# Last row pair of a Strassen-Winograd matmul kernel: another order of the seven products, the residual put into a PSUM bank, and the last copies split over two engines

## Chip, cores and metric

The kernel runs on one core of a Trainium2 chip. The metric is the device time of one execution in microseconds (us). Three runs of the kernel before gave 866.5, 866.58 and 866.75 us, so the median is 866.58 us.

## What is computed

With x of 2048 rows (tokens) by 640 columns (channels):

```python
xn = layernorm(x)                                   # over the 640 channels
a, b = xn @ dft_hid_re.T, xn @ dft_hid_im.T
A = dft_seq_re @ a - dft_seq_im @ b                 # real part of a 2-D Fourier transform
h = layernorm(xn)
u = gelu(einsum("sd,sf->df", h, w1) + b1)           # f = 1728, mixing across tokens
B = (u @ w2 + b2).T                                 # back to 2048 rows, 640 columns
out = x + A + B
```

All in float32. The last stage, which the change touches, is the product with `w2`.

## The kernel before

**Arithmetic.** Each matmul of float32 operands is done in three passes (`three`, L158). An operand is split into a rounded part hi and a rest lo: ScalarE writes hi with a copy (`high`, L149) and VectorE writes lo with a subtraction (`low`, L152). The passes are hi by hi, hi by lo (L161, L162) and lo by hi (L164).

**Row pairs.** The stages after the sequence transform all go through `row_steps` (L851). It takes two rows of tiles of the left matrix at a time and computes a 2 by 2 block of results with seven products instead of eight (Strassen-Winograd). The left matrix comes as four pieces A11, A12, A21, A22; the sums S1 = A21 + A22, S2 = S1 - A11, S3 = A11 - A21 and S4 = A12 - S2 are made by VectorE (`first_sum`, and `s2`, `s3`, `s4` at L1002). The right matrix with its own sums is in SBUF already (`moving`). In the last stage, `down(1, t)` (L1113), a piece is 128 by 384: three chunks of 128 inner indices. The result block is two tiles of 128 output rows by two halves of 320 columns, called c00, c01, c10, c11 here (row, half). Products 2, 3 and 4 are *stacked*: their last inner chunk has only 64 real rows, so its lo is put on the other 64 partitions and its third pass is left out. Such a product has 8 matmuls of 320 columns, the others have 9. For S4 the lower 64 partitions of that chunk are first made a copy of the upper ones by ScalarE, in `fourth` (L990).

**Banks.** P1 to P7 are the products; each goes into a PSUM bank, and some share one: P1, P6 and P7 accumulate one after another in bank z, P5 and P3 in bank y, P2 has bank w, and P4 has bank u in the last pair. Between two products of one bank the intermediate sum is read out (`read`, L922). c01 is P1 + P6, then + (P5 + P3). c11 is (P5), then + (P1 + P6 + P7). c10 is (P1 + P6 + P7), then + P4. c00 is P1 + P2.

**Order of the work.** The schedule is manual: each engine executes its instructions in the order in which the program text issues them. A *step* is one product; `turn_of(i)` (L1224) issues for step i, in this order: loads, reads of the banks that step i - 1 filled, sums, the hi of the piece for step i + 2 (ScalarE), extras, the lo of that piece (VectorE), the list `behind_lo`, and last the matmuls of step i (TensorE). A piece has three buffers. So operands are two steps ahead of TensorE, and a product's bank is read one step behind it. In what follows s is the first step of the last row pair, and turn s + n the turn of its step n.

**The last row pair** is `down(1, 7)`, with `base` given: the 256 rows of the output so far (x + A + half of B), which is read into a buffer beforehand (`before`, L1128), and added to each result by VectorE, so that the final values are written by plain DMAs (`each`, L1122) and not by accumulating ones. Its order before is 1, 5, 2, 6, 3, 7, 4. Its sums are placed by L1005 to L1009: S2 behind the lo of turn s - 1; S4 and then S3 behind the lo of turn s; `fourth` behind the lo of turn s + 1. Its reads are: P1 copied to c00 by ScalarE (L962); c11 = P5 + base (L958); c00 += P2 (L949); c01 = P1 + P6 + base (L958); c01 += P5 + P3 (L949), and c00 += base (L975); c11 += bank z (L949), and c10 = bank z + base (L979); last c10 += P4, in two halves of 160 columns (L954), of which one is stored from SyncE's queue and one from ScalarE's.

Of the kernel before, what the change touches and what calls it, by code (L numbers as in the profile page):

```python
# [14 lines left out]
P = 128  # L15
# [12 lines left out]
H2 = D // 2  # L28
# [49 lines left out]
def fnet_plus_mixer(  # L78
# [30 lines left out]
    nc = tc.nc  # L109
# [35 lines left out]
    for i in range(WARM):  # L145
        n = CH if i < WARM - 5 else P
# [8 lines left out]
    def sub(to, a, b):  # L155
        nc.vector.tensor_sub(to, a, b)  # L156
# [11 lines left out]
    def bank():  # L168
        bank_turn[0] = (bank_turn[0] + 1) % 8
        return psum[bank_turn[0]]  # L170
# [6 lines left out]
    loads, sums, reads, extras, timed, behind_lo = (defaultdict(list) for _ in range(6))  # L177
# [115 lines left out]
    def pair_at(tag):  # L293
        return keep.tile([P, 2, D], F32, name="pair", tag=tag)
# [3 lines left out]
    def part_of(tag, n):  # L298

        def get():  # L300
            if tag not in shared:
                shared[tag] = keep.tile([P, 3, 2, D], F32, name="pairs", tag=tag)
            return shared[tag][:, n]
        return get

    place = {
        "v": lambda: pair_at("v"), "ca": lambda: pair_at("ca"), "cb": lambda: pair_at("cb"),
        "x0": part_of("xb", 0), "x1": part_of("xb", 1), "x2": part_of("xb", 2),
    }
# [536 lines left out]
    def raw_slot(n):  # L846
        k = n if n == D else CH
        raw_turn[k] = (raw_turn[k] + 1) % (raws[k].shape[1] - 1)
        return raws[k][:, raw_turn[k], :n]

    def row_steps(stage, nq, load_piece, at, end, bias=(None, None), base=None, earliest=0, each=None, aside={}, tail=False, stacked=()):  # L851
# [6 lines left out]
        s0, n = len(steps), nq * P  # L858
        raw, banks, held = {}, {}, {}
# [19 lines left out]

        order = (1, 5, 2, 6, 3, 7, 4) if base else (1, 5, 6, 2, 7, 3, 4)

        early = n < D
        loads_of = {-6: ("A11", "A21", "A22"), -4: ("A12",)} if early else {
# [2 lines left out]
        operand = {1: "A11", 5: "s", 6: "A11", 2: "A12", 7: "A21", 3: "A12", 4: "A22"}  # L888
# [7 lines left out]
        new_bank = (1, 5, 2)  # L896
# [2 lines left out]
            new_bank += (7, 3)  # L899
        if base:  # L900
            bank_of[4] = "u"
            new_bank += (4,)
        of_moving = {1: 0, 2: 1, 3: 2, 5: 3, 7: 4, 4: 5, 6: 6}

        goes_to = {1: (0, 0, True), 5: (1, 1, True), 6: (0, 1, True), 2: (0, 0, False), 7: (1, 1, False),
# [16 lines left out]
        def read(i):  # L922
            def run():
                if i == 1:
                    held["c"] = place[at]()
                row, half, fresh = goes_to[i]
                cols = slice(half * H2, (half + 1) * H2)
                c, b = held["c"][:, row, cols], banks[bank_of[i]][:, :H2]
                if tail and i in (5, 7, 4):

                    def upper():
                        aside[i](row, half, b)
                        if i == 4:
                            end(held["c"])


                    if i == 7:
                        upper()
                    else:
                        extras[s0 + (4 if i == 5 else order.index(i) + 1)].append(upper)  # L940
                    if i == 5:
                        nc.scalar.activation(c, b, AF.Copy)
                    else:
                        nc.vector.tensor_add(c[:TAIL], b[:TAIL], c[:TAIL])
                    return
                if i in aside:
                    aside[i](row, half, b)
                elif not fresh:
                    nc.vector.tensor_add(c, b, c)  # L949
                elif base and i == 4:  # L950

                    for k, queue in enumerate((nc.sync, nc.scalar)):
                        of = slice(k * H2 // 2, (k + 1) * H2 // 2)
                        nc.vector.tensor_add(c[:, of], b[:, of], c[:, of])  # L954
                        each(c, row, half, True, of, queue)
                    return
                elif base and i != 1:
                    nc.vector.tensor_add(c, b, base()[:, row, cols])  # L958
                elif bias[row] is not None:
                    nc.scalar.activation(c, b, AF.Identity, bias=bias[row])  # L960
                else:
                    nc.scalar.activation(c, b, AF.Copy)  # L962
                if tail and i == 6:

                    low_row = held["c"][:, 1, :]
                    nc.vector.tensor_add(low_row[:, H2:], b, low_row[:, H2:])
                    extras[s0 + 3].append(lambda: nc.scalar.activation(low_row[:, :H2], b, AF.Copy))
                    p5 = banks["u"][:TAIL, :H2]
                    behind_lo[s0 + 3].append(lambda: nc.vector.tensor_add(c[:TAIL], p5, c[:TAIL]))
                if each:  # L970
                    each(c, row, half, i in (7, 3, 4))
                if base and i == 3:

                    c11 = held["c"][:, 0, :H2]
                    nc.vector.tensor_add(c11, c11, base()[:, 0, :H2])  # L975
                    each(c11, 0, 0, True)
                if base and i == 7:

                    nc.vector.tensor_add(held["c"][:, 1, :H2], b, base()[:, 1, :H2])  # L979
                if i == 4 and not each:  # L980
                    end(held["c"])
            return run

        if stacked:

            def second_time():
                last = raw["s"][:, n - P :]
                nc.scalar.activation(last[TAIL:], last[:TAIL], AF.Copy)

            def fourth():  # L990

                last = raw["A12"][:, n - P :]
                nc.scalar.activation(last[TAIL:], last[:TAIL], AF.Copy)

            if not base:
                extras[s0 + 1].append(second_time)
        for e, names in loads_of.items():
            loads[max(s0 + e, earliest)].append(lambda names=names: load(*names))
        if n == D or stacked:

            operand[6] = "s"
            s2 = lambda: sub(raw["s"], raw["s"], raw["A11"])  # L1002
            s3 = lambda: sub(raw["A21"], raw["A11"], raw["A21"])
            s4 = lambda: sub(raw["A12"], raw["A12"], raw["s"])
            if base:  # L1005
                sums_of = {-2: (first_sum,)}
                behind_lo[s0 - 1].append(s2)
                behind_lo[s0].extend((s4, s3))
                behind_lo[s0 + 1].append(fourth)  # L1009
            elif stacked:  # L1010
                sums_of = {-2: (first_sum,), 2: (s4,)}
                behind_lo[s0 - 1].append(s2)
                extras[s0].append(s3)
            elif s0 == s_hid:

                behind_lo[s0 - 2].append(first_sum)
                sums_of = {0: (s2,), 1: (s3,), 2: (s4,)}
            else:
                sums_of = {-2: (first_sum, s3), 2: (s4,)}
                behind_lo[s0 - 1].append(s2)  # L1020
        elif stage == "down0":

            sums_of[-2] = sums_of[-2][:1]
            behind_lo[s0 - 2].append(lambda: sub(raw["A21"], raw["A11"], raw["A21"]))
# [11 lines left out]
    def hidden(n, t, earliest):  # L1036
        ts = (t, t + 4)

        def load_piece(to, i, j):
            c, b = divmod(ts[i], CH // P)  # L1040
            nc.sync.dma_start(to.rearrange("p (j t) -> p j t", j=ND), y_part[j][c][:, :, b * P : (b + 1) * P])

        return row_steps("hid", ND, load_piece, ("ca", "cb")[n % 2] if n else "c", lambda c: collect(c, ts), earliest=earliest)

    def up(stage, r, at):
# [60 lines left out]
        if tail:  # L1106
            aside += (5, 7, 4)
        s0 = row_steps(
            f"up{stage}", 4, load_piece, at, end, earliest=s_up - 4, aside={i: by_dram(i) for i in aside}, tail=tail,
        )  # L1110
# [137 lines left out]
    with tc.manual_schedule():  # L1248
        for word in START.split():
            start[word[0]](*map(int, word[1:].split("-")))  # L1250
        for i in range(FIRST_STEP, len(steps) + 1):
# [6 lines left out]
            elif i >= s_hid:  # L1258
                k = sum(i >= s for s in (s_up, s_up + 7 * NF2, s_down))
                at, of = LONG_AT[k]  # L1260
# [43 lines left out]
```

## Time and profile before

| | |
|---|---|
| median of 3 runs | 866.58 us (866.5 to 866.75) |
| profiled execution: span from first to last instruction | 865.1 us |
| profiled execution: own time | not recorded apart from the span |
| TensorE busy | 860.7 us, 99% of the span |
| VectorE busy | 695.2 us, 80% |
| ScalarE busy | 523.0 us, 60% |
| granted TensorE clock | 1.000 |

The profile names engines PE (TensorE), PEld (its weight loads), DVE (VectorE), ACT (ScalarE), POOL (GpSimd) and SP (SyncE); a q behind a name is that engine's queue. A timeline row reads: start in us, busy us, engine, line of the kernel, operation, output <- input, shapes, how many instructions are merged in the row (x), and in brackets how long the engine sat idle before it and what ended that. The seven products of the last pair are 60 matmuls (four products of 9, three of 8).

### The profile page before, as it was taken

What the parts mean: (1) busy time and instruction counts of PE and PEld (TensorE: products, weight loads), DVE (VectorE), ACT (ScalarE), POOL (GpSimd) and SP (SyncE); (2) the same over time, 40 slices, a digit from 0 to 9 for tenths busy, and PEclk for the clock granted to TensorE, in tenths of its full rate; (3) what the DMA queues carried; (4) which work ended last, traced back from release to release, by engine and by line L of the source; (5) the groups of instructions that cost most, each with busy time, mean ns of one, the idle gap of its engine ahead of it and who ended that gap; (6) DMA issues with size and microseconds to landing.
All of it is one profiled execution on the core that took longest, in us unless ns stands there. A gap on an engine that the chain in (4) does not pass through costs nothing.

```text
span 865.1 us, 13904 instructions
## 1 busy us (share of the span) xinstructions
PE 860.7 (99%) x4899; PEld 789.6 (91%) x4899; DVE 695.2 (80%) x1177; ACT 523.0 (60%) x968; POOL 158.8 (18%) x215
## 2 busy tenths in 40 slices
PE   9999999999999999999999999999999999999998
PEld 6888888888888888889999999999999999999998
DVE  7898868758767888677877788888679978987887
ACT  5765576763555555547565556676667866555654
POOL 2222131210020211122110101111312221101211
PEclk9999999999999999999999999999999999999999
DMA  9949596695382746869576766665687689766776
GB/s 337 366 103 268 186 245 235 160 292 151 94 191 29 199 102 135 212 107 200 125 167 157 163 138 196 189 173 162 142 185 176 146 241 244 183 141 126 157 170 149
DMA packets 90293, 154.44 MB, mean 179 GB/s; under 512 B 9008, under 2 KB 37424, under 8 KB 89968
## 3 DMA queue, kind: packets, MB, share of 16 engines
q0 software_dynamic: 25008, 57.52, 36.1%
q1 hardware_dynamic: 64928, 95.80, 34.0%
q8 instruction: 38, 0.62, 0.3%
q10 hardware_dynamic: 288, 0.25, 0.1%
q14 instruction: 31, 0.25, 0.1%
HBM read 99.96 MB, written 58.82 MB: 184 GB/s over the span
## 4 chain that ended last, share of the span: by engine, by line
PE 99%; DMA 1%; SPq 0%; ACT 0%; DVE 0%; issue 0%; DVEq 0%
PE psum L161 32%; PE psum L162 32%; PE psum L164 31%; PE psum L515 3%; DMA pieces<-in_dft_seq 1%; ACT piece L150 0%; SPq L503 0%; SPq L539 0%; DVE pair L954 0%; DVEq L1300 0%
## 5 line engine op out<-in xcount | busy, mean ns | idle before, releaser
L153 DVE TENSOR_TENSOR piece<-pieces,piece 128x512 fp32r<-128x512 f32 (+4 forms) x496 | 327.2, 660 | 129.8 <-ACT piece L150 125.2
L150 ACT ACTIVATE piece<-pieces 128x512 fp32r<-128x512 f32 (+3 forms) x472 | 295.3, 626 | 224.6 <-PE psum L164 143.0
L161 PE MATMUL psum<-piece,n 128*128 128x512 f32 x540 | 210.3, 389 | 0.0
L164 PE MATMUL psum<-piece,n 128*128 128x512 f32 x540 | 210.3, 389 | 0.0
L162 PE MATMUL psum<-piece,n 128*128 128x512 f32 x540 | 210.3, 389 | 0.0
L162 PE MATMUL psum<-sup,piece 128*128 128x320 f32 x392 | 120.9, 309 | 0.0
L162 PE MATMUL psum<-sdown,piece 128*128 128x320 f32 x392 | 120.9, 309 | 0.0
L161 PE MATMUL psum<-sup,piece 128*128 128x320 f32 x392 | 120.9, 309 | 0.0
L161 PE MATMUL psum<-sdown,piece 128*128 128x320 f32 x392 | 120.9, 309 | 0.0
L162 PEld LDWEIGHTS psum<-piece,n 128*128 128x128 f32 x540 | 101.4, 188 | 21.1
L161 PEld LDWEIGHTS psum<-piece,n 128*128 128x128 f32 x540 | 101.4, 188 | 20.9
L164 PEld LDWEIGHTS psum<-piece,n 128*128 128x128 f32 x540 | 101.4, 188 | 20.9
L156 DVE TENSOR_TENSOR pieces<-pieces 128x512 f32<-128x512 f32 (+3 forms) x142 | 111.9, 793 | 3.0
L164 PE MATMUL psum<-sup,piece 128*128 128x320 f32 x368 | 113.9, 310 | 0.0
L164 PE MATMUL psum<-sdown,piece 128*128 128x320 f32 x368 | 113.9, 310 | 0.0
L492 POOL DMA_DIRECT2D y<-c x65 | 56.0, 898 | 255.2 <-DVE c L691 154.0
L164 PE MATMUL psum<-shid,piece 128*128 128x320 f32 x280 | 86.7, 310 | 0.0
L162 PE MATMUL psum<-shid,piece 128*128 128x320 f32 x280 | 86.7, 309 | 0.0
L161 PE MATMUL psum<-shid,piece 128*128 128x320 f32 x280 | 86.6, 309 | 0.0
L161 PEld LDWEIGHTS psum<-sdown,piece 128*128 128x128 f32 x392 | 73.6, 188 | 0.0
L161 PEld LDWEIGHTS psum<-sup,piece 128*128 128x128 f32 x392 | 73.6, 188 | 0.0
L162 PEld LDWEIGHTS psum<-sup,piece 128*128 128x128 f32 x392 | 73.6, 188 | 0.0
(135 smaller groups left out, 1107.2 us busy)
## 6 DMA issues: line engine op xcount, KB each, us to landing
pieces<-in_dft_seq SPq DMA_DIRECT2D x120, 256.0 KB, 5.4
y<-c POOLq DMA_DIRECT2D x105, 256.0 KB, 4.9
pieces<-in_w SPq DMA_DIRECT2D x88, 256.0 KB, 3.8
out<-pair POOLq DMA_DIRECT2D x36, 320.0 KB, 5.5
pieces<-y SPq DMA_DIRECT2D x32, 320.0 KB, 4.2
pieces<-in_w SPq DMA_DIRECT2D x32, 192.0 KB, 2.6
out<-in_x SPq DMA_DIRECT2D x16, 320.0 KB, 8.8
up<-pair POOLq DMA_DIRECT2D x8, 640.0 KB, 3.2
```

The costliest lines, as they stand in the source:

```text
L150: nc.scalar.activation(hi, src, AF.Copy)
L153: nc.vector.tensor_sub(lo, src, hi.bitcast(F32))
L156: nc.vector.tensor_sub(to, a, b)
L161: nc.tensor.matmul(psum, wh, mh, start=first, stop=False, skip_group_check=True)
L162: nc.tensor.matmul(psum, wh, ml, start=False, stop=last and wl is None, skip_group_check=True)
L164: nc.tensor.matmul(psum, wl, mh, start=False, stop=last, skip_group_check=True)
L492: nc.gpsimd.dma_start(y_part[m][c][:, j, :], t, accum_op=ALU.add)
L515: nc.tensor.matmul(banks[m, j], channels(k, j)[rows], w[cols], start=n == 0 and k == begin, stop=n == 2 and k == end, skip_group_check=True,)
```

## The change

Only the last row pair (`base`) changes.

- The order becomes 1, 5, 6, 3, 7, 4, 2: P6 moves one step forward to step 2, P3 to step 3, P7 to step 4, P4 to step 5, and P2 goes from step 2 to the end.
- S4 is put in a raw slot of its own instead of over A12, since P2 now needs A12 later than P3 needs S4. It stays behind the lo of turn s, and `fourth`, which now works on the new slot, follows it at once in turn s. S3 moves behind the lo of turn s + 1.
- After P1 has been copied to c00, VectorE writes c00 + base into bank w, behind the lo of turn s + 2 (`seed`). P2 then accumulates onto that (w is no longer among the banks that its first matmul starts anew), so bank w ends as the final c00. The addition of P2 to c00 (L949) and the addition of base to c00 (L975) are gone.
- c10 += P4 is one addition of 320 columns, stored from SyncE's queue, one turn before the end.
- The last thing is now the read of bank w: VectorE copies its first 160 columns to c00, stored from SyncE's queue, and ScalarE copies the other 160 to a place in another buffer, stored from ScalarE's queue.

```diff
-        order = (1, 5, 2, 6, 3, 7, 4) if base else (1, 5, 6, 2, 7, 3, 4)
+        order = (1, 5, 6, 3, 7, 4, 2) if base else (1, 5, 6, 2, 7, 3, 4)
...
         if base:
             bank_of[4] = "u"
-            new_bank += (4,)
+            new_bank = (1, 5, 4)
+            operand[3] = "S4"
...
+                if base and i == 2:
+                    apart = place["x0"]()[:, 0, :H2]
+                    for k, (queue, copy, to) in enumerate(((nc.sync, nc.vector.tensor_copy, c), (nc.scalar, high, apart))):
+                        of = slice(k * H2 // 2, (k + 1) * H2 // 2)
+                        copy(to[:, of], b[:, of])
+                        each(to, row, half, True, of, queue)
+                    return
                 if i in aside:
                     aside[i](row, half, b)
-                elif not fresh:
+                elif not fresh or base and i == 4:
                     nc.vector.tensor_add(c, b, c)
-                elif base and i == 4:
-
-                    for k, queue in enumerate((nc.sync, nc.scalar)):
-                        of = slice(k * H2 // 2, (k + 1) * H2 // 2)
-                        nc.vector.tensor_add(c[:, of], b[:, of], c[:, of])
-                        each(c, row, half, True, of, queue)
-                    return
...
-                if base and i == 3:
-
-                    c11 = held["c"][:, 0, :H2]
-                    nc.vector.tensor_add(c11, c11, base()[:, 0, :H2])
-                    each(c11, 0, 0, True)
...
+                if base and i == 1:
+                    banks["w"] = bank()
+
+                    def seed():
+                        nc.vector.tensor_add(banks["w"][:, :H2], c, base()[:, row, cols])
+
+                    behind_lo[s0 + 2].append(seed)
...
-                last = raw["A12"][:, n - P :]
+                last = raw["S4" if base else "A12"][:, n - P :]
                 nc.scalar.activation(last[TAIL:], last[:TAIL], AF.Copy)
...
+            def s4_apart():
+                raw["S4"] = raw_slot(n)
+                sub(raw["S4"], raw["A12"], raw["s"])
+
             if base:
                 sums_of = {-2: (first_sum,)}
                 behind_lo[s0 - 1].append(s2)
-                behind_lo[s0].extend((s4, s3))
-                behind_lo[s0 + 1].append(fourth)
+                behind_lo[s0].extend((s4_apart, fourth))
+                behind_lo[s0 + 1].append(s3)
```

## Prediction

> **What bounds the kernel now.** I read the page first, then the end of the trace engine by engine. The page:
>
> ```profile
> span 865.1 us, 13904 instructions
> PE 860.7 (99%) x4899; PEld 789.6 (91%) x4899; DVE 695.2 (80%) x1177; ACT 523.0 (60%) x968; POOL 158.8 (18%) x215
> PE 99%; DMA 1%; SPq 0%; ACT 0%; DVE 0%; issue 0%; DVEq 0%
> ```
>
> TensorE is busy for 99% of the span, and the chain that ended last is TensorE throughout. The change leaves the number of matmuls alone, so it can act in two ways only: by making TensorE wait, and through the tail behind the last matmul. Time for three runs is given, none for the profiled execution; its span is 1.48 us below their median (866.58 - 865.1), and I add what changes in the span to 866.58. One per five hundred (1.73 us) is about what can be told from no change here.
>
> TensorE in the last row pair, the first and last of 48 matmuls, and the view by stretches:
>
> ```profile
> 854.72 0.31 PE L161 MATMUL psum<-sdown,piece 128*128 128x320 f32 x1
> ...
> 861.61 0.31 PE L162 MATMUL psum<-sdown,piece 128*128 128x320 f32 x1
> ```
> ```profile
> 855.00:863.00 8.00, 6.92 (x48) 6.66 (x46) 6.84 (x18) 2.22 (x5) 0.21 (x1) 1.00 0.72 142
> ```
>
> 47 intervals in 6.89 us are 0.1466 us a matmul, without a gap, at clock 1.00: a product of 9 lasts 1.32, one of 8 lasts 1.17. Counted back from 861.61 the products begin at 852.96 (P1), 854.28 (P5), 855.60, 856.77, 858.09, 859.26, 860.58. VectorE is busy 6.84 of these 8.00 us, so it has little room to catch up: what matters is when its queue gets to an instruction.
>
> VectorE and ScalarE around the last pair (the pair before it, for the order that the change takes over, begins 8.8 us earlier):
>
> ```profile
> 844.89 1.03 DVE L156 TENSOR_TENSOR pieces<-pieces 128x384 f32<-128x384 f32 x2
> 846.10 0.56 DVE L153 TENSOR_TENSOR piece<-pieces,piece 128x384 fp32r<-128x384 f32 x1 [0.18 <-ACT piece L150]
> ...
> 850.34 0.73 DVE L153 TENSOR_TENSOR piece<-pieces,piece 64x128 fp32r<-64x128 f32 x2
> 850.99 0.48 DVE L949 TENSOR_TENSOR pair<-psum,pair 128x320 f32<-128x320 f32 x1
> ...
> 852.23 0.56 DVE L153 TENSOR_TENSOR piece<-pieces,piece 128x384 fp32r<-128x384 f32 x1
> 852.71 0.48 DVE L949 TENSOR_TENSOR pair<-psum,pair 128x320 f32<-128x320 f32 x1
> 853.11 0.55 DVE L153 TENSOR_TENSOR piece<-pieces,piece 128x384 fp32r<-128x384 f32 x1
> 853.69 0.56 DVE L156 TENSOR_TENSOR pieces<-pieces 128x384 f32<-128x384 f32 x1
> ...
> 855.04 1.03 DVE L156 TENSOR_TENSOR pieces<-pieces 128x384 f32<-128x384 f32 x2
> ...
> 856.45 0.48 DVE L958 TENSOR_TENSOR pair<-psum,pair 128x320 f32<-128x320 f32 x1
> ...
> 858.48 0.48 DVE L958 TENSOR_TENSOR pair<-psum,pair 128x320 f32<-128x320 f32 x1
> ...
> 859.64 0.49 DVE L949 TENSOR_TENSOR pair<-psum,pair 128x320 f32<-128x320 f32 x1
> 860.04 0.48 DVE L975 TENSOR_TENSOR pair<-pair 128x320 f32<-128x320 f32 x1
> ...
> 861.96 0.56 DVE L954 TENSOR_TENSOR pair<-psum,pair 128x160 f32<-128x160 f32 x2 [0.28 <-PE psum L162]
> ```
> ```profile
> 845.54 0.53 ACT L150 ACTIVATE piece<-pieces 128x384 fp32r<-128x384 f32 x1 [0.74 <-DVE pieces L156]
> ...
> 846.83 0.31 ACT L988 ACTIVATE pieces<-pieces 64x128 f32<-64x128 f32 x1
> 847.16 0.44 ACT L962 ACTIVATE pair<-psum 128x320 f32<-128x320 f32 x1
> 847.49 0.52 ACT L150 ACTIVATE piece<-pieces 128x384 fp32r<-128x384 f32 x1
> ...
> 854.48 0.44 ACT L962 ACTIVATE pair<-psum 128x320 f32<-128x320 f32 x1 [0.47 <-PE psum L164]
> 854.81 0.52 ACT L150 ACTIVATE piece<-pieces 128x384 fp32r<-128x384 f32 x1
> 855.63 0.31 ACT L993 ACTIVATE pieces<-pieces 64x128 f32<-64x128 f32 x1 [0.30 <-DVE pieces L156]
> ...
> 862.55 0.35 ACTq L1124 DMA_DIRECT2D out<-pair  x1
> ```
>
> Both engines run in the order of the text: 854.48 is the read of P1, 854.81 the hi of S2, 855.63 `fourth`, as `turn_of` issues them. Banks z and y are read in good time: P1 by 854.92, before P6 accumulates onto z at 856.77; P5 from 856.45 to 856.93, before P3 at 858.09; P1 + P6 from 858.48 to 858.96, before P7 at 859.26. In the new order each of these has one product less in between.
>
> **The change part by part.** I follow the two queues from S2 at 853.69, up to which nothing differs. Each step is the distance between two starts of the same kind in the rows above.
>
> The hi of S2 now comes first on ScalarE. S2 to its hi is 0.65 (844.89 to 845.54): 854.34. Hi to lo 0.56 (845.54 to 846.10): lo of S2 at 854.90. S4 follows, 0.48 behind a lo where it does not wait for it (852.23 to 852.71; 0.58 where it does, 853.11 to 853.69; S4 has a slot of its own, so I take the first): 855.38. `fourth` starts 0.59 behind S4 (855.04 to 855.63): 855.97. It stands ahead of the read of P1 in ScalarE's queue, so what is queued behind its wait is this read, and behind that the hi of S4; TensorE waits for both. Read 0.33 behind it (846.83 to 847.16): 856.30, for 0.44, until 856.74. P6 is due at 855.60. What a restart costs is seen at the kernel's beginning only:
>
> ```profile
> 6.54 0.63 ACT L150 ACTIVATE piece<-pieces 128x512 fp32r<-128x512 f32 x1 [1.57 <-DMA pieces<-in_dft_seq]
> ...
> 7.23 0.73 PE L515 MATMUL psum<-piece,n 128*128 128x512 f32 x2 [0.27 <-ACT piece L150]
> ```
>
> 7.17 to 7.23, so 0.06. P6 starts at 856.80: **first wait 1.20 us**.
>
> Hi of S4 0.33 behind the read (847.16 to 847.49): 856.63; lo, as above, 0.56 later: 857.19; S3 0.65 behind the two parts of a stacked lo (850.34 to 850.99): 857.84. Only then does VectorE's queue reach the read of P5, 0.48 later (two subtractions in 1.03 of 0.56 each): 858.32, until 858.80. P3 onto bank y would begin at 856.80 + 1.32 = 858.12; it begins at 858.86: **second wait 0.74**. Its own operand (lo of S4, done by 857.92) is no longer late.
>
> Hi of S3 at 857.84 + 0.65 = 858.49, lo at 859.05, then the added seed at 859.53, an addition of 128x320 for which I take the row of its kind, to the next instruction 0.40 (859.64 to 860.04, nothing of a write into a bank is in the trace; 0.48 at most, its busy time). The read of P1 + P6 starts at 859.93, until 860.41. P7 would begin at 858.86 + 1.17 = 860.03 and begins at 860.47: **third wait 0.44**. P7's lo is there by 859.61.
>
> From there TensorE sets the pace again: P7, P4 and P2 begin at 860.47, 861.79 and 862.96. VectorE meanwhile does the lo of A22 (by 861.2), adds P3 to c01, does the lo of A12 (by 862.3), adds P7 twice and P4 once, all before the last matmul at 862.96 + 7 x 0.1466 = 863.99, which is 2.38 later than 861.61. The removed additions (0.48 for P2, 0.48 for base) and the moved P4 addition save nothing, since they lay beside TensorE's work or come again (the seed, 0.48). The extra S4 slot costs nothing: its last reader is the pair before. The seed is done by 860.0, and P2 at 862.96 does not wait for it. If I take 0.58 for the two places behind a lo, the sum grows by 0.20; with 0.59 in place of 0.65 at the two hi it falls by 0.12: 2.26 to 2.58.
>
> The tail. Before, VectorE starts 0.35 behind the last matmul's start, and the last store is issued by ScalarE at 862.55, 0.94 behind it. Now two engines read one bank. The trace has one such place, in the earlier stage:
>
> ```profile
> 687.75 0.43 ACT L962 ACTIVATE pair<-psum 128x320 f32<-128x320 f32 x1
> ...
> 688.21 0.49 DVE L966 TENSOR_TENSOR pair<-psum,pair 128x320 f32<-128x320 f32 x1 [0.18 <-ACT pair L962]
> ```
>
> These two read the same bank into different places, and VectorE waits until ScalarE has ended (688.18). So I take it that the second copy waits for the first. Durations, from the view of groups by shape:
>
> ```profile
> L954 DVE TENSOR_TENSOR pair<-psum,pair 128x160 f32<-128x160 f32 x2 | 0.6, 320 | 0.3 <-PE psum L162 0.3
> ```
> ```profile
> L150 ACT ACTIVATE n<-x 128x128 fp32r<-128x128 f32 x1 | 0.3, 314 | 0.0
> ```
>
> VectorE's copy 0.32 at most; ScalarE's lies between 0.31 (128 columns) and 0.44 (320), 0.33 for 160. One after the other, with 0.06 and 0.03 between: 0.35 + 0.32 + 0.06 + 0.33 + 0.03 = 1.09 to the last store, 0.15 more than now. Side by side it would be 0.71, 0.23 less. The Trainium skill, PSUM — Partial Sum Buffer, section "PSUM bank collisions raise a hardware error", says that two engines must not read one bank at once either, so that whoever orders the instructions keeps them apart; by it the tail is the +0.15, against -0.23 for the two copies as the change words them, and the wait at 688.21 agrees.
>
> Store sizes change little: c10 goes as one of 160 KB, shortly ahead of the last two.
>
> ```profile
> out<-pair SPq DMA_DIRECT2D x3, 160.0 KB, 1.8
> out<-pair SPq DMA_DIRECT2D x1, 80.0 KB, 1.6
> ```
>
> It lands 0.2 later than one of 80 KB; I price that at 0, because it is issued by about 863.7 and the last two near 865, and keep 0.2 as upper bound.
>
> **Sum.** 1.20 + 0.74 + 0.44 = 2.38, and 0.15: +2.5 us, 869.1. Own range 866.58 + 2.26 - 0.23 = 868.6 to 866.58 + 2.58 + 0.15 + 0.2 = 869.5.
>
> **Rivals.** *Only the first wait counts.* If VectorE takes the reads of P5 and of P1 + P6 as soon as their banks are full, the second and third wait go; P7's third matmul, due at 859.29 + 0.29, then still waits 0.09 for its lo (859.61, and 0.06). 1.20 + 0.09 + 0.15 gives 868.0, within one per five hundred. Against it stands that VectorE's rows follow the text everywhere in this pair. 10%.
>
> *Not slower: nothing waits.* If the read of P1 were ahead of `fourth` in ScalarE's queue (done by 855.3 then), and VectorE's two reads came before the lo of S4 and the seed, TensorE would run through and only the tail would move: 866.35 to 866.73. It decides at 855.60, 856.92 and 858.09, where P6, P3 and P7 are due: each read must have ended 0.06 earlier. The pair before shows P6 in this place without a wait, but its `second_time` (846.83) has an operand that was long there, while `fourth` waits for S4. If only the read of P1 came early, the second wait would grow to about 1.6 and the total stay above 2. 7%, and 2% for faster by over 0.2% by something that I don't see.
>
> *The clock falls.* If the waits made the throttle lower TensorE's clock to a half, the 25 matmuls of P7, P4 and P2 would take 3.7 us more (25 x 0.1466): 872.8.
>
> ```profile
> 864.20:864.50 0.30, 0.00 (x0) 0.00 (x0) 0.00 (x0) 0.00 (x0) 0.00 (x0) 1.00 0.00 0
> 864.50:864.80 0.30, 0.00 (x0) 0.00 (x0) 0.00 (x0) 0.00 (x0) 0.00 (x0) 0.71 0.00 0
> ```
>
> The granted clock is still 1.00 more than 2.2 us after the last matmul, and my longest wait is 1.20. 3%. [...]
>
> **How the numbers follow.** The sum of waits has 78%, the first wait alone 10%, no wait 7%, the clock 3%, faster 2%. Slower is 78 + 3 = 81%, within 0.2% 17%, faster 2%. The range runs from just under the first-wait case, 867.9, to 869.8, a little above the sum's upper end since each distance is rounded; outside lie the clock, no wait, faster and some 7% of the likeliest case.
>
> **What would show it.** In the changed trace: `fourth` near 855.97 and the read of P1 behind it; TensorE idle three times in the last pair, ahead of P6 (released by ScalarE's L962), P3 and P7 (both by VectorE's L958), 1.2, 0.7 and 0.4 us; VectorE idle ahead of the lo of S4 for over a microsecond; ScalarE's last copy starting where VectorE's ends. TensorE without a gap at 855.6 would prove the argument wrong, and so would a longest wait in front of P4 or P2.

## The result and the profile after

The changed kernel takes 869.39 us (median of 7 runs, 869.31 to 869.57) beside 866.67 us (7 runs, 866.50 to 867.11) for the kernel before: 2.72 us more, a ratio of 1.003 with a 95% interval of 1.0021 to 1.004. It is slower by 0.3%, and the interval lies clear of 1. The profiled execution took 869.57 us, its span is 867.8 us against 865.1.

First the page. Busy times have hardly moved, the span has:

```profile
span 867.8 us, 13900 instructions
PE 861.8 (99%) x4899; PEld 789.9 (91%) x4899; DVE 694.9 (80%) x1176; ACT 523.4 (60%) x969; POOL 158.8 (18%) x215
PE 98%; DVE 1%; ACT 0%; issue 0%; DVEq 0%; ACTq 0%
```

The chain that ended last, the third line, now has 1% on VectorE: it leaves TensorE somewhere. The timeline of TensorE shows where; it has three idle times, all ahead of the first matmul of a product. The lines before and behind each are shown with it:

```profile
855.37 0.31 PE L164 MATMUL psum<-sdown,piece 128*128 128x320 f32 x1
856.76 0.42 PE L161 MATMUL psum<-sdown,piece 128*128 128x320 f32 x1 [1.08 <-ACT pair L963]
857.02 0.32 PE L162 MATMUL psum<-sdown,piece 128*128 128x320 f32 x1
...
858.04 0.31 PE L164 MATMUL psum<-sdown,piece 128*128 128x320 f32 x1
858.90 0.39 PE L161 MATMUL psum<-sdown,piece 128*128 128x320 f32 x1 [0.55 <-DVE pair L959]
859.12 0.30 PE L162 MATMUL psum<-sdown,piece 128*128 128x320 f32 x1
...
859.99 0.31 PE L162 MATMUL psum<-sdown,piece 128*128 128x320 f32 x1
860.51 0.38 PE L161 MATMUL psum<-sdown,piece 128*128 128x320 f32 x1 [0.21 <-DVE pair L959]
860.73 0.31 PE L162 MATMUL psum<-sdown,piece 128*128 128x320 f32 x1
...
864.10 0.31 PE L162 MATMUL psum<-sdown,piece 128*128 128x320 f32 x1
```

These are P6, P3 and P7, released by the read of P1 (L963 is L962 of the kernel before), of P5 and of P1 + P6 (both L959, before L958). The idle time in brackets counts from the end of the last busy bar, which is 0.31 us long though the next matmul would start after 0.147. What the wait costs is the distance of starts beyond 0.147: from 855.37 to 856.76 that is 1.24 us, from 858.04 to 858.90 0.71, from 859.99 to 860.51 0.37. And the first matmul after a wait is followed only 0.26, 0.22 and 0.22 us later, not 0.147: another 0.11, 0.07 and 0.07. Together 2.57 us. (The last matmul begins at 864.10 instead of 861.61, 2.49 later, in a trace that up to S2 runs 0.07 us earlier: 2.56.)

The clock plays no part, by the view of stretches, whose third figure from the end is the granted clock (through the waits, and then after the last matmul):

```profile
855.40:864.40 9.00, 7.17 (x44) 6.18 (x43) 6.52 (x16) 2.62 (x6) 0.00 (x0) 1.00 0.52 104
866.20:866.50 0.30, 0.00 (x0) 0.00 (x0) 0.00 (x0) 0.00 (x0) 0.00 (x0) 1.00 0.45 124
866.50:866.80 0.30, 0.00 (x0) 0.00 (x0) 0.00 (x0) 0.00 (x0) 0.00 (x0) 0.62 0.00 0
```

The two queues, by the timelines of ScalarE and of VectorE:

```profile
854.27 0.53 ACT L150 ACTIVATE piece<-pieces 128x384 fp32r<-128x384 f32 x1 [0.75 <-DVE pieces L156]
855.89 0.31 ACT L996 ACTIVATE pieces<-pieces 64x128 f32<-64x128 f32 x1 [1.09 <-DVE pieces L156]
856.27 0.44 ACT L963 ACTIVATE pair<-psum 128x320 f32<-128x320 f32 x1
856.60 0.52 ACT L150 ACTIVATE piece<-pieces 128x384 fp32r<-128x384 f32 x1
858.44 0.94 ACT L150 ACTIVATE piece<-pieces 128x384 fp32r<-128x384 f32 x2 [1.32 <-PE psum L164]
...
864.81 0.30 ACT L150 ACTIVATE pairs<-psum 128x160 f32<-128x160 f32 x1 [3.90 <-DVE pair L951]
865.14 0.35 ACTq L1132 DMA_DIRECT2D out<-pairs  x1
```
```profile
853.62 0.56 DVE L156 TENSOR_TENSOR pieces<-pieces 128x384 f32<-128x384 f32 x1
854.83 0.56 DVE L153 TENSOR_TENSOR piece<-pieces,piece 128x384 fp32r<-128x384 f32 x1 [0.65 <-ACT piece L150]
855.30 0.55 DVE L156 TENSOR_TENSOR pieces<-pieces 128x384 f32<-128x384 f32 x1
857.15 0.73 DVE L153 TENSOR_TENSOR piece<-pieces,piece 64x128 fp32r<-64x128 f32 x2 [1.30 <-ACT piece L150]
857.80 0.55 DVE L156 TENSOR_TENSOR pieces<-pieces 128x384 f32<-128x384 f32 x1
858.27 0.48 DVE L959 TENSOR_TENSOR pair<-psum,pair 128x320 f32<-128x320 f32 x1
859.00 0.56 DVE L153 TENSOR_TENSOR piece<-pieces,piece 128x384 fp32r<-128x384 f32 x1 [0.25 <-ACT piece L150]
859.47 0.50 DVE L980 TENSOR_TENSOR psum<-pair 128x320 f32<-128x320 f32 x1
859.88 0.49 DVE L959 TENSOR_TENSOR pair<-psum,pair 128x320 f32<-128x320 f32 x1
...
864.45 0.32 DVE L951 COPY pair<-psum 128x160 f32<-128x160 f32 x1 [0.68 <-PE psum L162]
```

ScalarE stands idle for 1.09 us ahead of `fourth` (L996), which starts at 855.89, as soon as S4 (855.30 to 855.85) is there. The read of P1 stands behind it in the queue, though P1's bank has been full since about 854.4. VectorE stands idle 1.30 us ahead of the lo of S4 (857.15), with the read of P5 (858.27) two instructions behind that; P5 was finished by 855.7. The seed (L980) takes 0.50 us, and the next instruction starts 0.41 after the seed's start.

The view of the chain that ended last shows which of these decide the time. In the last pair it reaches TensorE only at P7 (860.51). Before that it goes through S2, its hi and lo, S4, 0.34 of "issue" where `fourth` runs, the read of P1, the hi and lo of S4, and from there:

```profile
857.88 0.48 DVE pieces L156
858.44 0.53 ACT piece L150
859.00 0.56 DVE piece L153
859.56 0.41 DVE psum L980
859.97 0.41 DVE pair L959
```

These are S3, its hi and lo, the seed, and the read of P1 + P6, which releases P7. The read of P5 is not among them: it holds up P3, but by these rows P7 would begin no earlier if the read of P5 alone were in time. No run moves that read alone.

At the end ScalarE starts its copy at 864.81, when VectorE's ends (864.77). ScalarE's store, the last one, is issued 1.04 us behind the start of the last matmul; before it was 0.94. So 2.57 of waits with restarts and 0.10 of tail make 2.67 of the 2.72 us measured.

### The profile page after: what moved, and what is told of

Same layout as the page of the kernel before. It is cut to its first block, busy times and chain, and to the rows that moved or that the text cites. A ratio compares the mean times of both kernels' runs of the same rounds, so it can differ in the third digit from the quotient of the medians.

```text
span 867.8 us, 13900 instructions
## 1 busy us (share of the span) xinstructions
PE 861.8 (99%) x4899; PEld 789.9 (91%) x4899; DVE 694.9 (80%) x1176; ACT 523.4 (60%) x969; POOL 158.8 (18%) x215
## 4 chain that ended last, share of the span: by engine, by line
PE 98%; DVE 1%; ACT 0%; issue 0%; DVEq 0%; ACTq 0%
PE psum L161 32%; PE psum L162 32%; PE psum L164 31%; PE psum L515 3%; PE psum L147 1%; DVE piece L153 0%; DVE pieces L156 0%; ACT piece L150 0%; DVE pair L957 0%; DVE pieces L874 0%; ACT pair L963 0%; DVE psum L980 0%; DVE pair L959 0%; DVE pair L951 0%; ACT pairs L150 0%
## 5 line engine op out<-in xcount | busy, mean ns | idle before, releaser
L161 PEld LDWEIGHTS psum<-sdown,piece 128*128 128x128 f32 x392 | 73.6, 188 | 2.6 <-ACT pair L963 1.3
L161 PEld LDWEIGHTS psum<-sup,piece 128*128 128x128 f32 x392 | 73.6, 188 | 0.0
L162 PEld LDWEIGHTS psum<-sdown,piece 128*128 128x128 f32 x392 | 73.6, 188 | 0.0
```

What stands on the lines that cost most here:

```text
L161: nc.tensor.matmul(psum, wh, mh, start=first, stop=False, skip_group_check=True)
L162: nc.tensor.matmul(psum, wh, ml, start=False, stop=last and wl is None, skip_group_check=True)
```

## Experiments

**Theory.** Three waits in a row follow from the order in two queues: the chain S2, hi, lo, S4, `fourth`, read of P1, hi and lo of S4, S3 and behind it the read of P5, hi and lo of S3, seed, read of P1 + P6. **Rivals.** The late read of P1 is the loss, and the others only show it again; or the loss is in the seed and the copies at the end. All kernels below start from the changed one. Each but one was timed in 5 to 11 runs alternating with the kernel before, whose median was 866.61 us beside the first four and 866.64 beside the others; the kernel with ScalarE's copy first ran once. The changed kernel was not timed again beside them, so a difference from its 869.39 us compares runs of different times, between which the kernel before differed by up to 0.06 us. Where a wait is given "by the starts", it is the distance between two starts of matmuls less 0.147.

### `fourth` behind the read of P1

```diff
-                behind_lo[s0].extend((s4_apart, fourth))
+                behind_lo[s0].append(s4_apart)
+                sums[s0 + 1].append(fourth)
```

> The changed kernel with one thing put elsewhere: fourth (the copy of S4's last chunk) stands behind the read of P1 in ScalarE's queue. Theory (the queues of VectorE and ScalarE make three waits in a row, and each follows from the chain S4, fourth, hi, lo, S3, read of P5): P6 begins on time, but the wait ahead of P3 grows from 0.71 to about 1.6 us, since the read of P5 still stands behind the lo of S4 and behind S3; P7 begins some 0.37 us earlier than in the changed kernel: 869.0 us. Rival (the late read of P1 is the loss): the first wait and its restart, 1.35 us, go and nothing takes their place: 868.0.

869.03 us (five runs, 868.9 to 870.98), 1.0035 times before (1.0023 to 1.0048). TensorE:

```profile
858.35 0.38 PE L161 MATMUL psum<-sdown,piece 128*128 128x320 f32 x1 [1.51 <-DVE pair L959]
859.96 0.39 PE L161 MATMUL psum<-sdown,piece 128*128 128x320 f32 x1 [0.21 <-DVE pair L959]
```

P6's wait is gone, and P3's has grown from 0.55 to 1.51 us by the brackets, from 0.71 to 1.68 by the starts (about 1.6 expected). Removing the largest of three waits brought 0.36 us out of 2.72: the read of P1 isn't the loss by itself. About as much, 0.37, the hi of S4 gains by no longer standing behind the read of P1: it starts 0.34 behind `fourth` instead of 0.71. The rival falls; the next wait in the chain had been hidden behind the first.

### S3 back behind S4

```diff
-                behind_lo[s0].extend((s4_apart, fourth))
-                behind_lo[s0 + 1].append(s3)
+                behind_lo[s0].extend((s4_apart, fourth, s3))
```

> The changed kernel with S3 back right behind S4 and fourth, ahead of the lo of S4 in VectorE's queue. Theory: VectorE does S3 in the gap in which it waits for the hi of S4, so the read of P5 comes 0.47 us earlier and the wait ahead of P3 falls from 0.71 to about 0.25, the one ahead of P7 from 0.37 to about 0.15: 868.7 us. Rival (the late read of P1 is the loss): the first wait stays and so does the time, 869.4.

868.68 us, 1.0024 (1.0015 to 1.0033). This is the 0.7 us less that was expected. By the starts the wait ahead of P3 is 0.24 us, as expected (0.25), and the one ahead of P7 only 0.02, where 0.15 was expected. S3 lies in the idle time ahead of the lo of S4, as VectorE's timeline shows, and the read of P5 follows the lo directly:

```profile
855.64 1.02 DVE L156 TENSOR_TENSOR pieces<-pieces 128x384 f32<-128x384 f32 x2
857.47 0.73 DVE L153 TENSOR_TENSOR piece<-pieces,piece 64x128 fp32r<-64x128 f32 x2 [0.81 <-ACT piece L150]
858.12 0.48 DVE L959 TENSOR_TENSOR pair<-psum,pair 128x320 f32<-128x320 f32 x1
```

So an instruction that stands a step "later" cost 0.7 us because it was moved out of an idle time to a place ahead of a read.

### The reads ahead of the lo of S4 and of the seed

```diff
+                late.add(s0 + 3)
...
-                    behind_lo[s0 + 2].append(seed)
+                    behind_lo[s0 + 3].append(seed)
...
-            ready[j] = steps[j][1]()
+            if j in late:
+                extras[i + 1].append(lambda: ready.update({j: steps[j][1]()}))
+            else:
+                ready[j] = steps[j][1]()
```

In the edit, `late` names the step whose lo is put off: the lo of S4 is issued one turn later, in the extras, and the seed one turn later too, so both stand behind a read.

> The changed kernel with the lo of S4 behind the read of P5, and the seed behind the read of P1 + P6, on VectorE; fourth stays ahead of the read of P1. Theory: the waits ahead of P3 and P7 go, the one ahead of P6 stays at 1.24 with a restart of 0.11: 868.15 us. Rival (the late read of P1 is the loss, the others only show it again): nothing changes, 869.4. Rival (the last copies are the loss): 869.4.

868.14 us, 1.0018 (1.0009 to 1.0027). Of the three idle times of TensorE one is left:

```profile
856.48 0.42 PE L161 MATMUL psum<-sdown,piece 128*128 128x320 f32 x1 [1.06 <-ACT pair L964]
```

With VectorE's reads in good time the late read of P1 costs its own wait and restart (1.22 + 0.10 by the starts in this trace) and no more.

### No seed

```diff
-            new_bank = (1, 5, 4)
+            new_bank = (1, 5, 4, 2)
...
-                    behind_lo[s0 + 2].append(seed)
+                    behind_lo[s0 + 5].append(lambda: nc.vector.tensor_add(c, c, base()[:, row, cols]))
...
-                        copy(to[:, of], b[:, of])
-                        each(to, row, half, True, of, queue)
+                        nc.vector.tensor_add(c[:, of], b[:, of], c[:, of])
+                        each(c, row, half, True, of, queue)
```

> The changed kernel without the seed: P2 begins a bank of its own, base is added to c00 in turn s + 5, and the last thing is c00 += P2 by VectorE in two halves, as the kernel before did with P4. Theory: the seed's 0.41 us lies on the way to the read of P1 + P6, so the wait ahead of P7 (0.37, and a restart of 0.07) goes, and the tail is 0.1 shorter: 868.85 us; the first two waits stay. Rival (seeding and the copies at the end cost nothing or are the loss): 869.4, or 866.7.

868.76 us, 1.0026 (1.0016 to 1.0035), 0.63 less than the changed kernel where 0.54 was expected. The waits ahead of P6 and P3 are as before this edit, P7 has none that the profile marks (0.03 by the starts):

```profile
856.56 0.42 PE L161 MATMUL psum<-sdown,piece 128*128 128x320 f32 x1 [1.07 <-ACT pair L962]
...
858.70 0.39 PE L161 MATMUL psum<-sdown,piece 128*128 128x320 f32 x1 [0.55 <-DVE pair L958]
```

The seed is 0.41 us of VectorE's queue on the way to a read that TensorE waits for. The same addition of base, in turn s + 5, makes TensorE wait nowhere. The edit also ends the kernel with two additions by VectorE, and the last store is issued 0.93 us behind the last matmul's start, as in the kernel before.

### The last copies: both by VectorE, and in the other order

Both by VectorE, then ScalarE's copy issued first:

```diff
-(nc.sync, nc.vector.tensor_copy, c), (nc.scalar, high, apart)
+(nc.sync, nc.vector.tensor_copy, c), (nc.scalar, nc.vector.tensor_copy, c)
```
```diff
-(nc.sync, nc.vector.tensor_copy, c), (nc.scalar, high, apart)
+(nc.scalar, high, apart), (nc.sync, nc.vector.tensor_copy, c)
```

> The changed kernel with both last copies by VectorE, into c00. Theory: the three waits stay as they are, the last store is issued 0.94 instead of 1.04 us behind the last matmul's start: 869.3 us. Rival (the tail is the loss): 867 or less.

> The changed kernel with the two last copies issued in the other order, ScalarE's first. Theory (two engines don't read one bank at once, whichever comes first): now ScalarE starts 0.35 us behind the last matmul and VectorE waits until ScalarE has ended; time as the changed kernel, 869.4 within 0.1 us. Rival (ScalarE is merely slower to start): both start together and the last store is issued 0.3 us earlier.

869.24 us (1.0031, 1.002 to 1.0043) and, in a single run, 869.31 us. The tail of the first, by VectorE and ScalarE's queue: two copies in 0.56 us, the last store 0.93 behind the start of the last matmul (863.92).

```profile
864.27 0.56 DVE L950 COPY pair<-psum 128x160 f32<-128x160 f32 x2 [0.68 <-PE psum L162]
```
```profile
864.85 0.35 ACTq L1131 DMA_DIRECT2D out<-pair  x1
```

That of the second, ScalarE and then VectorE:

```profile
864.21 0.30 ACT L150 ACTIVATE pairs<-psum 128x160 f32<-128x160 f32 x1 [3.52 <-PE psum L162]
```
```profile
864.55 0.33 DVE L951 COPY pair<-psum 128x160 f32<-128x160 f32 x1 [1.02 <-ACT pairs L150]
```

Whichever comes first, the other engine's copy is released by its end (ScalarE's copy ends at 864.51, VectorE's starts at 864.55). So in these kernels two engines read one bank one after the other; what the chip does where nothing makes the second one wait, no run here shows. Splitting the copy between two engines costs 0.1 us in the tail against leaving both to VectorE, whose second copy starts about 0.24 behind its first (0.56 for both, 0.32 for one). The times alone are too close together to show 0.1 us; the timelines carry this.

### All places moved

The order of products, the seed and (in the first of two) the last copies stay; five instructions stand elsewhere. Beside the two edits of the reads above:

```diff
-                behind_lo[s0 - 1].append(s2)
-                behind_lo[s0].extend((s4_apart, fourth))
-                behind_lo[s0 + 1].append(s3)
+                behind_lo[s0 - 1].extend((s2, s4_apart))
+                behind_lo[s0].append(s3)
+                sums[s0 + 1].append(fourth)
```

> The changed kernel with five places moved: S4 right behind S2 (ahead of the lo of S2), S3 behind the lo of turn s, fourth behind the read of P1, the lo of S4 behind the read of P5, the seed behind the read of P1 + P6. The order of products, the seed and the last copies stay as changed. Theory: each read and each operand is then in time by a few hundredths to tenths of a microsecond, TensorE has no wait in the last pair, and only the tail is 0.1 us longer than before: 866.8 us. Rival (the order of products, the seed or the last copies are the loss): still over 868.

> As the run with all places moved, and both last copies by VectorE, into c00. Theory: the second copy no longer waits for a handover between engines and starts about 0.24 us behind the first: last store issued about 0.94 us behind the last matmul's start, as before: 866.7 us. Rival (two engines side by side are faster): 0.2 us more than with two engines.

866.91 us (1.0003, 0.9994 to 1.0012) and 866.80 us (1.0, 0.9991 to 1.0009). The profile marks no idle time of TensorE in the last pair of either; by the starts two of its matmuls are late, together by 0.07 and 0.06 us. VectorE of the first:

```profile
853.27 1.15 DVE L156 TENSOR_TENSOR pieces<-pieces 128x384 f32<-128x384 f32 x2
854.48 0.56 DVE L153 TENSOR_TENSOR piece<-pieces,piece 128x384 fp32r<-128x384 f32 x1
854.95 0.55 DVE L156 TENSOR_TENSOR pieces<-pieces 128x384 f32<-128x384 f32 x1
855.42 0.48 DVE L960 TENSOR_TENSOR pair<-psum,pair 128x320 f32<-128x320 f32 x1
```

S4 is done in the time in which VectorE waited for the hi of S2, and the profile marks no idle time of VectorE up to the read of P5. So neither the order of products nor seeding a bank is slow in itself; where the operands and reads stand in the queues made the difference. Neither version can be told from the kernel before, so the change gains nothing either: the seeded bank leaves a copy where there was an addition at the end, and with both halves by VectorE either takes two instructions in 0.56 us.

## Why the prediction was right

*The two queues followed instruction by instruction.* This held: every start of the chain came within 0.04 us of the predicted one once the 0.07 us by which this trace runs earlier are taken off, from the hi of S2 (854.34 predicted, 854.27 in the trace) to the read of P1 + P6 (859.93 and 859.88). Distances taken from rows of the same kind carried over. For S4 and the seed, each behind a lo, the prediction chose 0.48 over 0.58; the trace has 0.47 for both.

*The three waits, 1.20, 0.74 and 0.44.* Right in place and releaser; they measured 1.24, 0.71 and 0.37, 0.06 less in sum. That an early read of P1 alone would enlarge the second wait to about 1.6 and leave the total above 2 was shown with `fourth` behind the read of P1: the wait is 1.68, and 869.03 us is 2.4 above before.

*The seed, 0.40 to the next instruction.* It measured 0.41, and the kernel without the seed shows that it lay on the path.

*The restart, 0.06.* Too small. Between release and start it held (the read of P1 ends at 856.71, P6 starts at 856.76), but the prediction had nothing for the first matmul after a wait, which delays the next by 0.11, 0.07 and 0.07 us. That is 0.25, more than the 0.19 between the sum (2.38 + 0.15 = 2.53) and the 2.72 measured. The waits and the tail were put 0.06 and 0.05 too high, so part of this miss cancelled by luck, and 0.05 us of the 2.72 stays unexplained.

*The tail, 0.15 longer.* It is 0.10 longer: ScalarE's copy took 0.30, not 0.33, and started 0.04 behind VectorE's end, not 0.06. The choice between 1.09 one after the other and 0.71 side by side, made by the row at 688.21, was right; that row is not the only such place, since the same line waits for ScalarE at 603.11 too. The trace agrees with the section of the Trainium skill named there (PSUM — Partial Sum Buffer, "PSUM bank collisions raise a hardware error") as far as the order goes: the two reads of one bank are kept apart, 0.04 us from one's end to the other's start, with either engine first.

*The rivals.* "Only the first wait counts" (868.0) is what the kernel with the reads ahead does, 868.14; it needed an order that the change doesn't have. "Nothing waits" (866.35 to 866.73) is what the kernel with all places moved comes near: 866.91 us, which is 0.27 above the kernel before, where 0.15 at most was given, with an interval of the ratio (0.9994 to 1.0012) that includes no change. The clock did not fall: the view of stretches has it at 1.00 through the waits, and lower only after 866.5, more than 2 us after the end of the last matmul.

## What to carry to other kernels

When an instruction is moved between in-order queues, follow what stands behind it: here a copy of 0.31 us that waited for its operand held back the read of a bank, and TensorE needed that bank for the next product. Write down when each bank is next accumulated onto and when its read comes up in its queue, not only when operands are ready. Waits that lie in a row can hide one another: here removing the largest brought 0.36 of 2.72 us, and nearly all came back only when the order of the whole chain was changed.

## What the runs showed of the hardware

In the changed kernel the first matmul after a wait of TensorE is followed 0.22 to 0.26 us later instead of 0.147, at a granted clock of 1.00. The delay does not grow with the wait: it is 0.07 us after waits of 0.71 and 0.37 us and, in the kernel with `fourth` behind the read of P1, after one of 1.68 us, and 0.08 us after one of 0.02 us in the kernel with S3 back behind S4, all ahead of P3 or P7, whose banks VectorE reads; it is 0.10 to 0.11 after the waits of P6 (1.21 to 1.24 us in six kernels), whose bank ScalarE reads. Whether that difference comes from the engine that reads the bank or from the product stays open. A VectorE addition of 128x320 that writes into a bank takes 0.49 to 0.50 us against 0.48 for one from SBUF into SBUF. A VectorE copy of 128x160 out of a bank takes as long as an addition of that shape, 0.32 us.
